# Linear attention before two mixtures of experts: keys and values laid out as head by 64 partitions

## The chip, the core and the metric

The kernel runs on one core of a Trainium2 chip. The metric is device time in microseconds, as the median of several executions. One execution is also recorded by the hardware profiler, and all rows below come from that recording. A core has a matrix engine (TensorE, PE in the rows, with its weight loads as PEld), a vector engine (VectorE, DVE), a scalar engine (ScalarE, ACT), GpSimd (POOL) and a synchronization engine (SyncE, SP) that hands out nearly all transfers. In this kernel PE's results stand in PSUM tiles and all other operands in SBUF tiles, both of up to 128 partitions.

## The reference

The inputs are float32: q, k and v of shape (4 batches, 8 heads, 576 tokens, 64), the weights of two gated layers, and domain probabilities.

```
q_s = exp(q - max over d);      q_s /= sum over d + 1e-9
k_s = exp(k - max over tokens); k_s /= sum over tokens + 1e-9
kv  = einsum('bhsd,bhse->bhde', k_s, v)
x   = einsum('bhsd,bhde->bhse', q_s, kv)      # then to (2304 tokens, 512)
y   = ((x @ w1) * (x @ w2)) @ w3 @ w_out
out = sum over 4 experts e of p[:, e] * (relu(y @ e1[e]) @ e2[e])
```

## The kernel before

All stages are in one program. A planner orders the instructions of each engine ahead of time, from the order in which the source emits them and from its own cost estimates; `hold` and `after_inst` add order edges by hand.

Attention works on pairs of heads. For a pair `(b, hp)`, `load_k` (L186, L189) brings 512 tokens as 128 partitions by four tokens for both heads side by side, and the other 64 tokens as a fifth row on 64 partitions. `load_v` does the same with a 65th column of ones, in which the sums over tokens come out. For the first batch (`V_WHOLE`) the values go through a raw buffer (L209) and a ScalarE copy (L212); for the others they are written straight into the padded tile, one transfer per head and one for the tail (L214, L217). `load_q` (L230) brings the queries as 64 partitions by nine tokens, in two transfers for each half.

`k_max` takes the maximum over the tokens of a partition on VectorE (L239, L243, L244), transposes it on PE (L246), reduces it to one column (L250), spreads that column over all partitions with a matmul against the identity (L252) and copies it out on ScalarE (L258). `k_exp` subtracts (L270) and exponentiates (L273), in two pieces, the 128-partition rows and the 64-partition tail.

`k_v` (batches 0 and 1, L294) multiplies both heads at once: five accumulating matmuls, 128 columns of weights against 130 moving columns, of which the off-diagonal blocks are thrown away. `k_v2` (batches 2 and 3, L321) does two pairs in one PSUM bank and keeps the heads apart: for each row r and head h a matmul with 64 columns of weights and 65 moving columns, so that head h writes partitions 64h to 64h+63. A float32 matmul is recorded as two passes, a transposition as one. The result is scaled into block-diagonal tiles (L308, L336), and `x_stage` (L405) applies it to the transposed queries.

Slots set the order. The first batch's attention comes ahead of all; slots 6 to 13 and 14 to 21 compute `ab_step` (L109 to L111) for the first two chunks of 512 tokens, slots 22 to 29 the product of w3 and w_out, later slots `y_step`. Batch 1's keys start at slots 6 to 9, batch 2's at 30 to 34, batch 3's at 46 to 50, between these matmuls. Meanwhile the weights, which arrive as 64-bit floats (L495), are turned into float32 on ScalarE and VectorE (`conv_abs`, L140, and `conv_rest`, L144 to L155) and split in two parts (L103, L104). The experts' layers follow (L976, L1053). In the first batch, `keep_busy` issues filler matmuls (L123).

Of the kernel before, what the change touches and what calls it, by code (L numbers as in the profile page):

```python
# [8 lines left out]
F32 = mybir.dt.float32  # L9
# [28 lines left out]
JOINED = 2  # L38
# [20 lines left out]
def linear_attention_moe_kernel(ctx: ExitStack, tc, q, k, v, w1, w2, w3, wo, dp, e1, e2, out):  # L59
# [11 lines left out]
    KR, KX = 4, S - 4 * P  # L71
# [122 lines left out]
    staged = {}  # L194

    def load_v(b, hp):
        t = ap_.tile([P, 2, KR + 1, D + 1], F32, tag="vt", name="vt", bufs=4)
        nc.gpsimd.memset(t[..., D:D + 1], 1.0)
        if b >= JOINED:
            nc.gpsimd.memset(t[KX:P, :, KR, 0:D], 0.0)  # L200
        src = v[b, 2 * hp:2 * hp + 2]
        if b in V_WHOLE:
            i = PAIRS.index(hp)
            if i % 2 == 0:
                staged[b] = raw("vs")
            x = staged[b][:, 512 * (i % 2):512 * (i % 2) + 512].rearrange(
                "p (h r d) -> p h r d", h=2, d=D
            )
            hold(("in", b), nc.sync.dma_start(  # L209
                out=x, in_=src[:, 0:KR * P].rearrange("h (p r) d -> p h r d", p=P)  # L210
            ))
            nc.scalar.activation(out=t[:, :, 0:KR, 0:D], in_=x, func=ACTF.Copy)  # L212
        for h in range(0 if b in V_WHOLE else 2):
            hold("pace" if b > 2 else ("in", b), nc.sync.dma_start(  # L214
                out=t[:, h, 0:KR, 0:D], in_=src[h, 0:KR * P].rearrange("(p r) d -> p r d", p=P)
            ))
        hold("pace" if b > 2 else ("in", b), nc.sync.dma_start(  # L217
            out=t[0:KX, :, KR, 0:D], in_=src[:, KR * P:S].rearrange("h p d -> p h d")
        ))
        vt[b, hp] = t  # L220
# [5 lines left out]
    def load_q(b, j):  # L226
        t = ap_.tile([P, 2, QR, D], F32, tag="qr", name="qr", bufs=2)
        for hh in range(2):
            h0 = 4 * hh + 2 * j
            hold("pace" if b > 2 else ("in", b), nc.sync.dma_start(  # L230
# [5 lines left out]
    def k_max(b, hp):  # L236
        kr = kraw[b, hp]
        m4 = ap_.tile([P, 2, 2, D], F32, tag="m2", name="m2", bufs=1)
        i = hold(("k", b, PAIRS.index(hp)), nc.vector.tensor_tensor(  # L239
            out=m4, in0=kr[:, :, 0:2], in1=kr[:, :, 2:4], op=ALU.max  # L240
        ))
        m2 = ap_.tile([P, 2, D], F32, tag="mf", name="mf", bufs=2)
        nc.vector.tensor_tensor(out=m2, in0=m4[:, :, 0], in1=m4[:, :, 1], op=ALU.max)  # L243
        nc.vector.tensor_tensor(out=m2[0:KX], in0=m2[0:KX], in1=kr[0:KX, :, KR], op=ALU.max)  # L244
# [4 lines left out]
        mt = ap_.tile([P, 1], F32, tag="mt", name="mt", bufs=2)  # L249
        nc.vector.tensor_reduce(out=mt, in_=ps[:, 0:P], axis=AX.X, op=ALU.max)  # L250

        i = nc.tensor.matmul(  # L252
            out=ps[:, P:2 * P], lhsT=mt.to_broadcast([P, P]), rhs=ident, start=True, stop=True
        )
        if b == 0:
            keep_busy(FILL_B[PAIRS.index(hp)], i)
        mx = ap_.tile([P, 2, 1, D], F32, tag="mx", name="mx", bufs=2)
        nc.scalar.activation(  # L258
# [921 lines left out]
```

## Time and profile before

| | |
|---|---|
| median of 3 executions | 1141.66 us (1141.65 to 1142.82) |
| the profiled execution | 1142.81 us, with a span of 1141.0 us from the first to the last instruction |
| mean granted TensorE clock over the span | 0.995 |
| PE busy | 1120.9 us, 98% of the span |
| VectorE busy | 869.1 us, 76% |
| ScalarE busy | 534.7 us, 47% |
| mean DMA rate | 270 GB/s |

The profiled execution's own time is 1.8 us above its span and 1.15 us above the median. Shares over the whole span are averages over stages with different limits. Matmul ends are modelled in the trace, so the time that a matmul takes in a stream is read from the start of one to the start of the next.

### The profile page before, as it was taken

Reading aid. Unit: us, or ns where it says so; the run is one execution under the profiler, and the core shown is the slowest. Engines: PE = TensorE matmul, PEld = TensorE weight load, DVE = VectorE, ACT = ScalarE, POOL = GpSimd, SP = SyncE. Lnnn points to the kernel's source line nnn. Section 1 sums busy time; section 2 is a strip of 40 time slices with the busy share of each in tenths; the row PEclk is TensorE's granted clock in tenths of the full one; section 3 lists DMA queues with packets and bytes.
Section 4 is the critical chain, followed back from the end, with each engine's and each line's share of the span. In section 5 each row is a group of like instructions: output and inputs, shape, how many; then the busy total and the mean of one; then the engine's idle time right before and its main releaser. Section 6 shows DMA issues by size and latency. Waiting matters only on the chain.

```text
span 1141.0 us, 18926 instructions
## 1 busy us (share of the span) xinstructions
PE 1120.9 (98%) x7159; PEld 1044.8 (92%) x7159; DVE 869.1 (76%) x1460; ACT 534.7 (47%) x974; POOL 11.4 (1%) x54
## 2 busy tenths in 40 slices
PE   7899999999999999999999999999999999999998
PEld 5677888878888889999999999999999999999998
DVE  7999696856565527999989997777779877777777
ACT  4775245745453326645555444444435434443441
POOL 0000000000010000000000000000000000000000
PEclk8999999999999999999999999999999999999999
DMA  9987962899989768777777888777777797777774
GB/s 266 269 334 289 294 174 83 222 339 396 338 283 396 301 240 311 285 281 272 290 262 289 290 305 289 248 256 251 253 253 249 251 307 249 254 251 250 253 246 128
DMA packets 124667, 308.04 MB, mean 270 GB/s; under 512 B 27936, under 2 KB 51488, under 8 KB 124576
## 3 DMA queue, kind: packets, MB, share of 16 engines
q1 hardware_dynamic: 123616, 306.04, 77.9%
q8 instruction: 57, 0.93, 0.3%
q10 hardware_dynamic: 960, 0.79, 0.3%
q14 instruction: 34, 0.28, 0.1%
HBM read 230.24 MB, written 76.55 MB: 269 GB/s over the span
## 4 chain that ended last, share of the span: by engine, by line
PE 91%; DVE 4%; DMA 3%; SPq 1%; issue 1%; ACT 0%; DVEq 0%; ACTq 0%
PE hp L976 30%; PE op L1053 29%; PE ab L111 5%; PE ab L110 5%; PE ab L109 5%; PE y L110 3%; PE y L111 3%; PE y L109 3%; PE W L109 1%; PE W L110 1%; PE W L111 1%; DMA eg<-e_b 1%; PE xp L405 1%; DMA vt<-in_v_dram 1%; PE kv L294 1%
## 5 line engine op out<-in xcount | busy, mean ns | idle before, releaser
L1053 PE MATMUL op<-eg,h 128*128 128x256 f32 x3024 | 379.8, 280 | 0.8 <-DMA eg<-e_b 0.8
L976 PE MATMUL hp<-t,eg 128*128 128x384 f32 x2016 | 376.9, 336 | 0.9 <-DVE acc L1034 0.9
L1053 PEld LDWEIGHTS op<-eg,h 128*128 128x128 f32 x3024 | 373.5, 188 | 1.2 <-PE hp L976 1.1
L976 PEld LDWEIGHTS hp<-t,eg 128*128 128x128 f32 x2016 | 344.6, 188 | 2.9 <-DVE acc L1034 1.8
L1034 DVE SCALAR_TENSOR_TENSOR acc<-op,prob,acc 128x256 f32<-128x256 f32 (+1 forms) x399 | 197.9, 525 | 42.0 <-PE op L1053 41.9
L103 ACT ACTIVATE h<-blk 128x768 fp32r<-128x768 f32 x168 | 138.0, 843 | 143.1 <-DVE blk L673 108.9
L104 DVE TENSOR_TENSOR h<-blk,h 128x768 fp32r<-128x768 f32 x168 | 157.2, 951 | 24.4 <-ACT h L103 24.3
L959 ACT ACTIVATE blk<-hp 128x384 f32<-128x384 f32 x192 | 90.4, 489 | 141.6 <-PE hp L976 138.1
L963 DVE TENSOR_TENSOR blk<-hp,blk 128x384 f32<-128x384 f32 x144 | 79.3, 556 | 67.0 <-PE hp L976 66.6
L109 PE MATMUL ab<-x,wg 128*128 128x512 f32 (+1 forms) x320 | 120.0, 378 | 1.5 <-ACT bd L308 1.1
L110 PE MATMUL ab<-x,wg 128*128 128x512 f32 (+1 forms) x320 | 118.6, 371 | 1.6 <-ACT x L426 1.4
L111 PE MATMUL ab<-x,wg 128*128 128x512 f32 (+1 forms) x320 | 117.9, 371 | 0.3 <-DVE wg L104 0.3
L965 ACT ACTIVATE blk<-blk 128x768 f32<-128x768 f32 x72 | 60.6, 845 | 73.0 <-DVE blk L963 71.3
L673 DVE TENSOR_TENSOR blk<-blk 128x768 f32<-128x768 f32 x96 | 91.4, 952 | 0.5
L110 PEld LDWEIGHTS ab<-x,wg 128*128 128x128 f32 x320 | 60.3, 189 | 13.1 <-ACT x L426 3.0
L109 PEld LDWEIGHTS ab<-x,wg 128*128 128x128 f32 x320 | 60.1, 189 | 12.7 <-ACT bd L308 1.3
L111 PEld LDWEIGHTS ab<-x,wg 128*128 128x128 f32 x320 | 60.3, 189 | 10.5 <-DVE wg L104 0.7
L567 DVE TENSOR_TENSOR ah<-ab,ah 128x512 f32<-128x512 f32 (+1 forms) x40 | 25.2, 631 | 39.3 <-PE ab L111 39.3
L104 DVE TENSOR_TENSOR eo<-e2r,eo 128x512 fp32r<-128x512 f32 x56 | 37.7, 683 | 20.0 <-ACT eo L103 19.8
L111 PE MATMUL y<-h,W 128*128 128x512 f32 x128 | 50.4, 397 | 0.0
L110 PE MATMUL y<-h,W 128*128 128x512 f32 x128 | 50.4, 394 | 0.0
L109 PE MATMUL y<-h,W 128*128 128x512 f32 x128 | 49.2, 401 | 0.0
(107 smaller groups left out, 1004.2 us busy)
## 6 DMA issues: line engine op xcount, KB each, us to landing
eg<-e_t SPq DMA_DIRECT2D x96, 512.0 KB, 4.5
eg<-e_b SPq DMA_DIRECT2D x72, 512.0 KB, 5.0
eg<-e_s SPq DMA_DIRECT2D x68, 512.0 KB, 4.4
eg<-e_a SPq DMA_DIRECT2D x51, 512.0 KB, 4.6
wg<-w SPq DMA_DIRECT2D x44, 512.0 KB, 8.3
f<-in_moe_w_dram SPq DMA_DIRECT2D x32, 512.0 KB, 6.7
e_t<-eo SPq DMA_DIRECT2D x32, 512.0 KB, 7.5
e_s<-eg SPq DMA_DIRECT2D x28, 512.0 KB, 4.5
```

The lines of the kernel that those rows point to most:

```text
L103: i = nc.scalar.activation(out=hi, in_=src, func=ACTF.Copy)
L104: j = eng.tensor_tensor(out=lo, in0=src, in1=hi.bitcast(F32), op=ALU.subtract)
L109: nc.tensor.matmul(out=ps, lhsT=w_hi, rhs=r_hi, start=first, stop=False, **kw)
L110: nc.tensor.matmul(out=ps, lhsT=w_hi, rhs=r_lo, start=False, stop=False, **kw)
L111: return nc.tensor.matmul(out=ps, lhsT=w_lo, rhs=r_hi, start=False, stop=last, **kw)
L673: return lambda: nc.vector.tensor_tensor(out=dst, in0=x, in1=y, op=op)
L959: nc.scalar.activation(out=block(name)[:, u], in_=src, func=func)
L963: nc.vector.tensor_tensor(out=x[:, u], in0=src, in1=x[:, u], op=ALU.add)
L965: nc.scalar.activation(out=x, in_=x, func=ACTF.Relu)
L976: nc.tensor.matmul(out=q, lhsT=w[:, sw, kt, P * u:P * u + P], rhs=t[b][:, kt, st], start=new and kt == 0 and i == 0, stop=kt == 1 and i == ...
L1034: nc.vector.scalar_tensor_tensor(out=dst, in0=src, scalar=prob[:, T, e:e + 1], in1=dst, op0=ALU.mult, op1=ALU.add,)
L1053: nc.tensor.matmul(out=q[:, c:c + DH], lhsT=g[:, sh, u, P * i:P * i + P], rhs=w[:, sw, u], start=new and u == 0 and j == 0, stop=u == 1 an ...
```

## The change

Keys and values are laid out as queries already are: a head takes 64 partitions, each with nine consecutive tokens, and the two heads of a pair lie on top of each other. One transfer brings the keys of a pair and one the values. The maximum over the nine tokens of a partition becomes one reduction with a stride of 64 elements. Its transposition fills 64 PSUM partitions instead of 128, the reduction to one column keeps the heads apart, and the spread takes two matmuls of 64 by 64. Subtraction and exponential become one instruction each. `k_v` and `k_v2` become one function for one or two pairs: for each of nine rows and each head, a matmul with 64 partitions of contraction, 64 columns of weights and 65 moving columns; head 0 uses partitions 0 to 63 and head 1 partitions 64 to 127, for the operands and for the result. The memsets for the tails go. The first batch's four query transfers are issued by ScalarE instead of SyncE.

```
     def load_k(b, hp):
-        t = ap_.tile([P, 2, KR + 1, D], F32, tag="kr", name="kr", bufs=4)
-        src = k[b, 2 * hp:2 * hp + 2]
+        t = ap_.tile([P, QR, D], F32, tag="kr", name="kr", bufs=4)
         hold("pace" if b > 2 else ("in", b), nc.sync.dma_start(
-            out=t[:, :, 0:KR], in_=src[:, 0:KR * P].rearrange("h (p r) d -> p h r d", p=P)
-        ))
-        hold("pace" if b > 2 else ("in", b), nc.sync.dma_start(
-            out=t[0:KX, :, KR], in_=src[:, KR * P:S].rearrange("h p d -> p h d")
+            out=t, in_=k[b, 2 * hp:2 * hp + 2].rearrange("h (p r) d -> (h p) r d", p=QP)
         ))
...
     def load_v(b, hp):
-        t = ap_.tile([P, 2, KR + 1, D + 1], F32, tag="vt", name="vt", bufs=4)
+        t = ap_.tile([P, QR, D + 1], F32, tag="vt", name="vt", bufs=4)
...
+        src = v[b, 2 * hp:2 * hp + 2].rearrange("h (p r) d -> (h p) r d", p=QP)
+        x = t[..., 0:D]
         if b in V_WHOLE:
...
+            x = raw("vs")[:, 0:QR * D].rearrange("p (r d) -> p r d", d=D)
+        hold("pace" if b > 2 else ("in", b), nc.sync.dma_start(out=x, in_=src))
+        if b in V_WHOLE:
+            nc.scalar.activation(out=t[..., 0:D], in_=x, func=ACTF.Copy)
...
-            hold("pace" if b > 2 else ("in", b), nc.sync.dma_start(
+            eng = nc.sync if b else nc.scalar
+            hold("pace" if b > 2 else ("in", b), eng.dma_start(
                 out=t[QP * hh:QP * hh + QP],
...
     def k_max(b, hp):
...
+        m2 = ap_.tile([P, D], F32, tag="mf", name="mf", bufs=2)
+        hold(("k", b, PAIRS.index(hp)), nc.vector.tensor_reduce(
+            out=m2, in_=kraw[b, hp].rearrange("p r d -> p d r"), axis=AX.X, op=ALU.max
         ))
...
-        i = nc.tensor.transpose(ps[:, 0:P], m2.rearrange("p h d -> p (h d)"), ident)
+        i = nc.tensor.transpose(ps[0:D, 0:P], m2, ident)
...
+        nc.vector.tensor_reduce(
+            out=mt, in_=ps[0:D, 0:P].rearrange("d (h p) -> d h p", h=2), axis=AX.X, op=ALU.max
+        )
+        for h in range(2):
+            i = nc.tensor.matmul(
+                out=ps[D * h:D * h + D, P:P + D], lhsT=mt[:, h].to_broadcast([D, D]),
+                rhs=ident[0:D, 0:D], start=True, stop=True,
+            )
...
+        mx = ap_.tile([P, 1, D], F32, tag="mx", name="mx", bufs=2)
+        nc.scalar.activation(out=mx[:, 0], in_=ps[:, P:P + D], func=ACTF.Copy)
...
+        t = ap_.tile([P, QR, D], F32, tag="ek", name="ek", bufs=2)
+        hold(("e", b, PAIRS.index(hp)), nc.vector.tensor_tensor(
+            out=kr, in0=kr, in1=mx.to_broadcast([P, QR, D]), op=ALU.subtract
+        ))
+        nc.scalar.activation(out=t, in_=kr, func=ACTF.Exp)
...
-    def k_v2(b, j):
...
+    def k_v(b, *pairs):
+        ps = bank(ps_w if b == 0 else ps_a, "kv").rearrange("p (w c) -> p w c", c=P)
+        n = len(pairs)
+        for w, hp in enumerate(pairs):
+            ek, vv, last = ekt.pop((b, hp)), vt.pop((b, hp)), None
+            for r in range(QR):
                 for h in range(2):
+                    p = slice(D * h, D * h + D)
                     i = nc.tensor.matmul(
-                        out=ps[D * h:D * h + D, hh, 0:D + 1], lhsT=ek[:, r, h], rhs=vv[:, h, r],
-                        start=r == 0, stop=r == KR, skip_group_check=hh > 0,
+                        out=ps[p, w, 0:D + 1], lhsT=ek[p, r], rhs=vv[p, r],
+                        start=r == 0, stop=r == QR - 1, skip_group_check=w > 0,
                     )
```

## Rows read from the trace of the kernel before

**Rows 1.** The page's first part: an engine's busy time, share of the span, instructions.

```profile
PE 1120.9 (98%) x7159; PEld 1044.8 (92%) x7159; DVE 869.1 (76%) x1460; ACT 534.7 (47%) x974; POOL 11.4 (1%) x54
```

**Rows 2.** Windows: length, each engine's busy time, granted clock, DMA share, GB/s.

```profile
3.60:16.00 12.40, 8.84 (x42) 5.95 (x41) 9.77 (x24) 3.55 (x9) 0.00 (x0) 0.89 0.96 248
16.00:46.90 30.90, 25.78 (x119) 19.11 (x118) 26.82 (x47) 23.06 (x60) 0.46 (x4) 0.88 1.09 283
46.90:75.00 28.10, 26.94 (x132) 21.70 (x131) 27.45 (x51) 21.39 (x70) 0.32 (x2) 1.00 1.04 355
75.00:92.00 17.00, 14.87 (x75) 11.31 (x74) 14.51 (x28) 11.21 (x28) 1.71 (x8) 1.00 0.60 227
92.00:340.00 248.00, 247.49 (x1251) 202.56 (x1250) 177.87 (x301) 125.19 (x255) 7.45 (x26) 1.00 0.81 271
```

**Rows 3.** Timeline of DVE, 3 to 36 us: start, us, instruction, idle before and releaser.

```profile
7.63 0.88 DVE L270 TENSOR_TENSOR kr<-kr,mx 128x512 f32<-128x512 f32 x2
8.43 0.27 DVE L244 TENSOR_TENSOR mf<-mf,kr 64x128 f32<-64x128 f32 x1
...
11.79 1.35 DVE L345 TENSOR_REDUCE qm<-qr 128x18 f32<-128x1152 f32 x1 [1.54 <-DMA qr<-in_q_dram]
...
17.93 0.16 DVE L301 TENSOR_SCALAR rs<-kv 128x1 f32<-128x1 f32 x1 [1.07 <-PE kv L294]
```

**Rows 4.** Timeline of SP's transfer issues, 0 to 110 us.

```profile
0.75 0.46 SPq L186 DMA_DIRECT2D kr<-in_k_dram  x1
...
5.94 2.56 SPq L230 DMA_DIRECT2D qr<-in_q_dram  x4
8.54 0.59 SPq L209 DMA_DIRECT2D vs<-in_v_dram  x1
```

**Rows 5.** Timeline of ACT, 0 to 17 us.

```profile
7.21 0.28 ACT L258 ACTIVATE mx<-mt 128x128 f32<-128x128 f32 x1 [4.86 <-PE mt L252]
```

**Rows 6.** DMA traffic of 8 to 12 us, then of 14 to 28 us.

```profile
DMA packets 476, 0.99 MB, mean 247 GB/s; under 512 B 47, under 2 KB 48, under 8 KB 476
...
DMA packets 5085, 4.68 MB, mean 335 GB/s; under 512 B 612, under 2 KB 5085, under 8 KB 5085
```

**Rows 7.** Groups of DVE by form, 0 to 46.9 us: busy, mean ns, idle before.

```profile
L345 DVE TENSOR_REDUCE qm<-qr 128x18 f32<-128x1152 f32 x3 | 4.0, 1344 | 1.5 <-DMA qr<-in_q_dram 1.5
...
L239 DVE TENSOR_TENSOR m<-kr 128x256 f32<-128x256 f32 x7 | 2.9, 411 | 3.7 <-DMA kr<-in_k_dram 3.7
L270 DVE TENSOR_TENSOR kr<-kr,mx 128x512 f32<-128x512 f32 x4 | 2.7, 678 | 0.0
...
L250 DVE TENSOR_REDUCE mt<-mt 128x1 f32<-128x128 f32 x5 | 1.4, 277 | 0.0
...
L270 DVE TENSOR_TENSOR kr<-kr,mx 64x128 f32<-64x128 f32 x4 | 1.1, 274 | 0.0
```

**Rows 8.** Instructions on the tile kv: duration min/median/max, first and last start.

```profile
L321 PE MATMUL kv<-vt,ek x160: 219/222/272, 181.0 to 301.5; 128*64 128x65 f32 x160
```

**Rows 9.** The chain that ended last, 198 to 204 us: start, us, what.

```profile
198.86 0.73 PE kv L321 x18
...
200.02 0.26 PE kv L321 x2
...
200.71 0.11 PE mt L246
...
203.10 0.22 PE mt L252 x2
```

**Rows 10.** Timeline of PE, 74 to 76.2 us and 232.5 to 234.8 us.

```profile
74.44 1.47 PE L294 MATMUL kv<-vt,ek 128*128 128x130 f32 x10
...
232.61 0.39 PE L110 MATMUL y<-h,W 128*128 128x512 f32 x1
232.93 1.39 PE L321 MATMUL kv<-vt,ek 128*64 128x65 f32 x40
...
234.59 0.40 PE L109 MATMUL y<-h,W 128*128 128x512 f32 x1
```

More of the change, by code (lines that the diff above doesn't have):

```diff
@@ L229, in load_q @@
             h0 = 4 * hh + 2 * j
-            hold("pace" if b > 2 else ("in", b), nc.sync.dma_start(
+            eng = nc.sync if b else nc.scalar
+            hold("pace" if b > 2 else ("in", b), eng.dma_start(
                 out=t[QP * hh:QP * hh + QP],
@@ L286, in empty_bd @@
         return bd_ring[-1]
-    def k_v(b, hp):
-        ek, vv = ekt.pop((b, hp)), vt.pop((b, hp))
-        bd = empty_bd()
-        ps = bank(ps_w if b == 0 else ps_a, "kv")
-        for r in range(KR + 1):
-            p = P if r < KR else KX
-            i = nc.tensor.matmul(
-                out=ps[:, 0:2 * D + 2], lhsT=ek[0:p, r].rearrange("p h d -> p (h d)"),
-                rhs=vv[0:p, :, r, :], start=r == 0, stop=r == KR,
-            )
-        if b == 0:
-            keep_busy(FILL_V[PAIRS.index(hp)], i)
-        rs = ap_.tile([P, 1], F32, tag="rs", name="rs", bufs=2)
-        nc.vector.tensor_scalar(
-            out=rs, in0=ps[:, D:D + 1], scalar1=1e-9, scalar2=None, op0=ALU.add
-        )
-        nc.vector.reciprocal(out=rs, in_=rs)
-        for h in range(2):
-            p = slice(D * h, D * h + D)
-            o = (D + 1) * h
-            nc.scalar.activation(
-                out=bd[p, D * h:D * h + D], in_=ps[p, o:o + D], func=ACTF.Copy, scale=rs[p]
-            )
-        kvb[b, hp] = bd
-    def k_v2(b, j):
-        ps = bank(ps_a, "kv").rearrange("p (w c) -> p w c", c=P)
-        bds, last = [], None
-        for hh in range(2):
-            bds.append(empty_bd())
-            ek, vv = ekt.pop((b, 2 * hh + j)), vt.pop((b, 2 * hh + j))
-            for r in range(KR + 1):
+    def k_v(b, *pairs):
[4 more added lines that the diff above has]
+            for r in range(QR):
                 for h in range(2):
+                    p = slice(D * h, D * h + D)
                     i = nc.tensor.matmul(
-                        out=ps[D * h:D * h + D, hh, 0:D + 1], lhsT=ek[:, r, h], rhs=vv[:, h, r],
-                        start=r == 0, stop=r == KR, skip_group_check=hh > 0,
+                        out=ps[p, w, 0:D + 1], lhsT=ek[p, r], rhs=vv[p, r],
+                        start=r == 0, stop=r == QR - 1, skip_group_check=w > 0,
                     )
@@ L327, in k_v2 @@
                     last = i
-        rs = ap_.tile([P, 2, 1], F32, tag="rs2", name="rs", bufs=2)
+        if b == 0:
+            keep_busy(FILL_V[PAIRS.index(hp)], i)
+        rs = ap_.tile([P, n, 1], F32, tag=f"rs{n}", name="rs", bufs=2)
         nc.vector.tensor_scalar(
-            out=rs, in0=ps[:, 0:2, D:D + 1], scalar1=1e-9, scalar2=None, op0=ALU.add
+            out=rs, in0=ps[:, 0:n, D:D + 1], scalar1=1e-9, scalar2=None, op0=ALU.add
         )
         nc.vector.reciprocal(out=rs, in_=rs)
-        for hh in range(2):
+        for w, hp in enumerate(pairs):
+            kvb[b, hp] = empty_bd()
             for h in range(2):
@@ L336, in k_v2 @@
                 nc.scalar.activation(
[L337 removed]
+                    out=kvb[b, hp][p, p], in_=ps[p, w, 0:D], func=ACTF.Copy, scale=rs[p, w]
                 )
[L339 removed]
     def q_exp(b, j):
@@ L456, in linear_attention_moe_kernel @@
             elif i % 2:
-                put(mid, s + 1, k_v2, b, i // 2)
+                put(mid, s + 1, k_v, b, PAIRS[i - 1], hp)
             at = s + (4 if b > 1 else 3)
```

50 lines of the change are left out of this document (1 added, 49 removed).

## The prediction

> **What bounds the kernel now.** I read the page's first part, then windows, then inside the stages the timelines, groups and chain. PE is busy for 98% of the span [rows 1], but a mean hides the start. The windows [rows 2] show four stages. From 3.6 to 46.9 us VectorE is busy for 36.59 of 43.30 us and PE has holes at a lower clock: attention of the first batch and the first weight conversions, in VectorE's order. From 46.9 to 75 us VectorE (27.45 of 28.10) and PE (26.94) are both nearly full. From 75 to 92 us PE misses 2.1 us. After that PE is the limit: in 92 to 340 us it lacks 0.51 us of 248, with VectorE at 72%. So a saving counts only up to about 92 us, where VectorE and the arrival of data set the pace; later everything that PE gains or loses goes to the end one for one. Batches 2 and 3 lie wholly in that later stage: their products run from 181 to 301 us [rows 8].
>
> **VectorE, per pair.** Durations come from [rows 7]. Before: 411 (L239), two of about 277 (L243, L244, like L250), 277 (L250), 678 and 274 (L270), in sum 2.19 us. After: one reduction over 576 elements, the small one, one subtraction over 576. Reductions cost 277 ns for 128 elements and 1344 for 1152, so 1.04 ns an element and 0.74 us for 576; subtractions 274 for 128 and 678 for 512, so 0.75 us for 576. With 0.28 that makes 1.77 us, 0.42 less. But durations overlap: the two L270 record 0.88 us and the next instruction starts 0.80 after them [rows 3], 0.08 per boundary, and three instructions fewer lose 3 x 0.08 of the gain. So 0.18 to 0.42 us, taken as 0.3. Batch 0 saves 4 x 0.3 = 1.2 us. Batch 1's 1.2 us falls mostly into 46.9 to 75, where PE is as full as VectorE and has only 1.16 us of holes [rows 2]; I count 0.4.
>
> No row has the stride of 64 elements. The reduction can't well be below the 0.74 us of a contiguous one; above, I take twice that. I choose 0.74, and the doubled price is a rival. The Trainium skill, "SBUF — State Buffer", section "Door 1: The DMA port swizzle", says that an access which moves on to another 16-byte line pays a penalty; no row here shows such a stride.
>
> **Transfers and queues.** SyncE now needs twelve issues before the first values: eight for keys from 0.75 us, four for queries from 5.94, so that the first value transfer goes at 8.54 [rows 4]. With four key transfers and the queries on ScalarE, at the same 0.64 us each (2.56 / 4), the values go at about 0.75 + 4 x 0.64 = 3.3 us and the first query at about 0.8 us. ScalarE's four issues cost 2.6 us and are hidden: before its first copy of the maximum, at 7.21 us, it has been idle for 4.86 [rows 5]. Without that cover they would add up to 2.6 us to the first pair's chain. Later batches save one key and two value issues a pair; PE doesn't wait there.
>
> What goes away are two of VectorE's waits [rows 3]: 1.54 us for the queries before 11.79 and 1.07 us for the first pair's product, which itself waits for values, before 17.93. Together 2.6 us. I count them fully, because queries and values are asked for over 5 us sooner. The first keys may land later, beside the queries; I set that against the short waits between the key transfers, at zero.
>
> DMA's share is 0.96 from 3.6 to 16 us and 1.09 to 46.9 [rows 2], so what comes earlier pushes other transfers back. The rate depends on the shape: 247 GB/s while query pieces of 2304 bytes dominate, 335 with pieces of 1 KB [rows 6]. New key and value transfers have pieces of 2304 bytes but all 128 partitions, where the queries have 64. By the slow rate 295 KB takes 1.19 us, by the other 0.88; over the twelve such transfers of the first two batches that is at most 12 x 0.31 = 3.7 us later at the end of this stage, and at least none. I take none, as the transfers that a wait names are the first ones. The Trainium skill, "SBUF — State Buffer", section "Door 1: The DMA port swizzle", has 64 partitions reach only half of the 16 ports, 128 all: by that rule the new layout isn't slow and the sum stays; if the size of the pieces were the cause, it would be up to 3.7 us worse. The trace holds no 2304-byte transfer on 128 partitions.
>
> So the start gains 1.2 + 0.4 + 2.6 = 4.2 us. Bounds: nothing, if the waits come back elsewhere or the planner's new order costs as much; and 10.1 us, all 6.7 us of VectorE's idle time to 46.9 (43.30 less 36.59 [rows 2]) and 8 x 0.42 of its work.
>
> **PE, the products of batches 2 and 3.** Here the work grows. Per function call the old code issues 2 pairs x 5 rows x 2 heads x 2 passes = 40, the new one 2 x 9 x 2 x 2 = 72: with 64 partitions a matmul covers half as many tokens. The chain gives 0.73 us for 18 passes and 0.26 for 2 [rows 9]: 0.47 / 16 = 29 ns a pass. A pass of L252 with 128 moving columns takes 0.11 us [rows 9], so 65 columns alone would take about 56 ns: the two heads run side by side, 58 ns for both. The new code keeps two heads on disjoint halves, so I keep 58. It needs 36 such steps for 20: 16 x 0.058 = 0.93 us a call, four calls, 3.7 us.
>
> Entering and leaving such a group costs too. Around the 40 passes the wide matmuls start at 232.61 and 234.59 [rows 10]: 1.98 us, less 0.46 for two wide ones at 0.23 each, less 20 x 0.058, leaves 0.36 us of overhead. Batch 1's product is a group of 36 passes now: 18 x 0.058 + 0.36 = 1.40 us, as against 1.47 [rows 10]; no change.
>
> **PE, the maximum.** The two passes of L252 take 0.22 us in the stream and the transposition 0.11 [rows 9], with no overhead visible. The spread becomes two 64-by-64 matmuls, thus a small group: 0.36 + 2 x 0.058 = 0.48 us, 0.26 more. Were there no overhead, it would be 0.11 less. The transposition has 64 columns of weights: between nothing and the same overhead, up to 0.3 more; between ends without a near row I take half, 0.15. Eleven pairs meet a full PE, eight of batches 2 and 3 and about three of batch 1: 11 x 0.41 = 4.5 us, bounds -1.2 and 6.2.
>
> Rescaling (L301, L329) and the copies to the diagonal keep their number. ScalarE's exponential and copy get about 0.3 us a pair shorter; ScalarE is at 74% before 46.9 and at half after, so that is worth nothing. The dropped memsets lie on GpSimd, busy 0.46 us of 30.9 [rows 2].
>
> **The sum.** 3.7 + 4.5 - 4.2 = +4.0 us, PE's part between 2.5 and 9.9, the start's between 0 and 10.1. Against the profiled execution, 1142.8 us with 1.8 around its span, this is 1146.8; that execution lies 1.15 us above the median, so against the median it is 1145.7. I forecast 1145.5 us, 0.3% slower. I call 0.2%, 2.3 us, the least that measurement can tell here.
>
> **Rivals.**
>
> A, the forecast: the start gains a few microseconds and PE pays about twice that. For it speak the windows after 92 us, where nothing can hide a longer PE. Chance 0.44, with times of 1143.5 to 1149.
>
> B, not slower: small groups pay no entry or exit where the maximum is spread and turned. Then PE's part is 2.5 us, the sum -1.7 and the time 1140.0. For it: L252 in the stream shows no overhead. Against: L321's groups do, at the same number of columns. It decides where the sum is zero: 11 x (1.5 x overhead - 0.10) = 0.5, at an overhead of 0.10 us a group, half of it counted for the transposition. Chance 0.22; it turns into faster if the start gains over 4.8 us.
>
> C, the start moves as a block: queries and values come over 5 us sooner and everything behind them follows, 5.3 us, with 2.4 of VectorE's work and the 2.1 us that PE lacks from 75 to 92, together 9.8. Less 8.2 for PE that is -1.6, 1140.1 us; with PE nearer to its lower bound it is below 1139.4 and faster. For it: the first product waits for its values. Against: VectorE is 87% busy from 16 to 46.9 us, and DMA is full. It decides at a gain of 8.2 us. Chance 0.18.
>
> D, the start gains about 1 us: either the strided reduction costs 0.74 us more (8 x 0.74 = 5.9, more than the gain), or keys land later beside the queries. Time 1141.7 + 8.2 - 1 = 1148.9. Chance 0.12.
>
> E, the two heads don't run side by side: 72 passes at 56 ns, 4.0 us instead of 20 x 0.058 = 1.2 a call, 11.5 for four, and 1.0 more for each of batch 1's four: 15.4 instead of 3.7, so about 1157 us. The Trainium skill, "TensorEngine Tiling (Array Packing)", section "Gotcha 1: PSUM Pressure", says that different row tiles can't access one PSUM bank at the same time, and here both heads' rows write one bank. Against it: they write different partitions of it, as the two heads do now, side by side. Chance 0.04.
>
> **Range and chances.** From C's faster part at about 1138.5 to D with some more, 1150; outside lie E and the ends of the bounds, under 2 in 10. Slower: 0.42 of A, 0.10 of D and E, 0.56. Faster: 0.09 of B and 0.13 of C, 0.22. Same: the rest of each, 0.22. The likeliest case's own range is 1143.5 to 1149.
>
> **What the profile would show.** The first query reduction starts well before 11.8 us, and no wait of 1 us for a product stands near 18. The reduction over 576 elements takes 0.74 us. In batches 2 and 3 a product has 72 passes with starts in pairs, 58 ns from pair to pair, and takes about 2.5 us in the stream. The spread takes 0.48 us instead of 0.22. The last hole of PE lies some 4 us earlier than 92. The prediction is wrong if the start gains more than 8 us, if the spread costs no more than before, or if the planner's new order opens holes in PE after 92 us.

## The result and the profile after

The changed kernel takes 1150.42 us (median of 6 runs, 1148.64 to 1153.40), the kernel before 1141.66 beside it (6 runs, 1141.24 to 1142.82): ratio 1.0078, 95% interval 1.0063 to 1.0092. It is slower by 8.8 us, where 3.8 were forecast, and 0.4 us outside the range. The profiled execution of after took 1149.19 us with a span of 1147.1. The traces thus differ by 6.4 us; the other 2.4 of the medians lie between executions of one kernel, and no trace locates them: the trace of before is the slowest of its six executions, that of after the second fastest, so by traces the new kernel looks a little better than it is.

I divide the trace by three events on TensorE: the first wide product (tile `ab`), the first product of `w_out` (W from `wg`), the first expert product (`hp`). In the expectations times count from a zero 0.24 us earlier: 108.77 there is 108.5 here; stretches are the same.

| | first `ab` | first W | first `hp` | W to `hp` |
|---|---|---|---|---|
| before | 32.3 | 108.8 | 424.3 | 315.5 |
| after | 34.8 | 108.5 | 430.3 | 321.8 |

From `hp` to the last product both take 711.5 to 711.7 us. So the start gained 0.3 us of the 3.0 forecast for it (4.2 less 3 x 0.41 for batch 1's maxima), and the stretch with batches 2 and 3 lost 6.3 of a forecast 7.0. The tiles W and `hp` of after, then of before; the last pair of numbers is the first and last start:

```profile
L108 PE MATMUL W<-wg x64: 388/389/500, 108.5 to 198.4; 128*128 128x512 f32 x64
```

```profile
L924 PE MATMUL hp<-t,eg x2016: 334/334/446, 430.3 to 1113.6; 128*128 128x384 f32 x184
```

```profile
L109 PE MATMUL W<-wg x64: 389/389/500, 108.8 to 198.0; 128*128 128x512 f32 x64
...
L976 PE MATMUL hp<-t,eg x2016: 332/334/445, 424.3 to 1107.9; 128*128 128x384 f32 x184
```

The page's first part and the windows of after, as [rows 1, 2]:

```profile
PE 1123.1 (98%) x7527; PEld 1044.4 (91%) x7527; DVE 874.2 (76%) x1412; ACT 532.3 (46%) x958; POOL 7.8 (1%) x38
```

```profile
3.60:16.00 12.40, 7.33 (x57) 4.25 (x57) 9.16 (x12) 3.35 (x7) 0.00 (x0) 1.00 1.06 288
16.00:46.90 30.90, 23.91 (x220) 17.48 (x217) 30.23 (x45) 21.32 (x54) 0.49 (x4) 0.94 1.07 307
46.90:75.00 28.10, 27.27 (x193) 21.58 (x191) 27.26 (x46) 23.23 (x75) 0.23 (x2) 1.00 1.00 333
75.00:92.00 17.00, 15.91 (x132) 12.59 (x131) 12.75 (x24) 10.22 (x24) 0.23 (x2) 1.00 0.57 206
92.00:340.00 248.00, 245.96 (x1360) 199.11 (x1359) 177.28 (x267) 118.84 (x236) 1.87 (x10) 1.00 0.78 262
```

VectorE's idle time from 3.6 to 46.9 us fell from 6.7 [rows 2] to 43.30 - 39.39 = 3.9 us, 2.8 us less where the forecast counted 2.6. But it is not the forecast's two waits that went. The one for the first product did (1.07 us); the one for the queries stayed (1.82 us, 1.54 before) and only stands 2.5 us earlier. The rest are mainly two waits for ScalarE, before 29.31 and 35.88 us of before's trace (0.95 and 1.09). That the sums agree is luck. The 2.8 us of work done sooner did not become time at W: from 75 to 92 us VectorE idles 4.25 us against 2.49. Its new groups up to 46.9 us (busy, mean ns, idle before) and its timeline, against [rows 3, 7]:

```profile
L218 DVE TENSOR_REDUCE mf<-kr 128x64 f32<-128x576 f32 x8 | 9.1, 1142 | 4.2 <-DMA kr<-in_k_dram 4.2
...
L243 DVE TENSOR_TENSOR kr<-kr,mx 128x576 f32<-128x576 f32 x5 | 3.7, 744 | 0.0
```

```profile
9.26 1.35 DVE L293 TENSOR_REDUCE qm<-qr 128x18 f32<-128x1152 f32 x1 [1.82 <-DMA qr<-in_q_dram]
...
18.16 0.15 DVE L277 TENSOR_SCALAR rs<-kv 128x1 f32<-128x1 f32 x1
...
19.69 0.68 DVE L143 TENSOR_SCALAR f<-f 128x1024 f32<-128x1024 f32 x1
```

Two rows of before's timelines, of VectorE and of ScalarE:

```profile
20.67 0.69 DVE L144 TENSOR_SCALAR f<-f 128x1024 f32<-128x1024 f32 x1
```

```profile
14.82 0.63 ACT L212 ACTIVATE vt<-vs 128x512 f32<-128x512 f32 x1 [3.86 <-DMA vs<-in_v_dram]
```

The subtraction costs the forecast 0.74 us. The strided reduction costs 1.14, not 0.74, so a pair records 2.16 us against 2.19: no saving. The first query reduction is 2.5 us earlier (11.79 before), the first conversion step L143 only 1.0 (20.67 before). In between stand arrivals. SyncE's issues (as [rows 4]), its own waits up to 60 us, and ScalarE's timeline:

```profile
0.74 2.23 SPq L184 DMA_DIRECT2D kr<-in_k_dram  x4
5.41 0.33 SPq L196 DMA_DIRECT2D vs<-in_v_dram  x1
...
9.18 2.76 SPq L196 DMA_DIRECT2D vs<-in_v_dram  x3
```

```profile
SPq L196 <- DMA qr<-in_q_dram: 6.1, 3, 2.4
```

```profile
13.78 0.68 ACT L198 ACTIVATE vt<-vs 128x576 f32<-128x576 f32 x1 [0.55 <-DMA vs<-in_v_dram]
...
20.45 0.69 ACT L139 ACTIVATE f<-f 128x512 f32<-128x512 f32 x1 [0.83 <-DMA f<-in_moe_w_dram]
...
30.05 1.25 ACT L139 ACTIVATE f<-f 128x512 f32<-128x512 f32 x2 [1.03 <-DVE wg L103]
31.18 1.16 ACT L312 ACTIVATE qe<-qr 128x1152 f32<-128x1152 f32 x1
32.37 0.49 ACT L342 ACTIVATE qT<-qt 128x384 f32<-128x384 f32 x1
```

With four key and four query transfers asked for, SyncE's next issue waits until a query has landed (the trace doesn't show why): the first values go at 5.41 us, not 3.3, the others from 9.18. Their first copy starts at 13.78, 1.0 us earlier than before (14.82), though they were asked for 3.1 us earlier; DMA's share there is 1.06. At 20.45 ScalarE waits for a weight.

On TensorE, around the last product call and around one spread of a maximum:

```profile
306.28 0.39 PE L110 MATMUL y<-h,W 128*128 128x512 f32 x1
306.60 2.32 PE L267 MATMUL kv<-vt,ek 64*64 64x65 f32 x72
308.84 0.50 PE L108 MATMUL y<-h,W 128*128 128x512 f32 x1
309.18 0.40 PE L109 MATMUL y<-h,W 128*128 128x512 f32 x1
```

```profile
211.58 0.39 PE L110 MATMUL y<-h,W 128*128 128x512 f32 x1
211.90 0.33 PE L230 MATMUL mt<-ident,mt 64*64 64x64 f32 x4
212.16 0.50 PE L108 MATMUL y<-h,W 128*128 128x512 f32 x1
212.50 0.40 PE L109 MATMUL y<-h,W 128*128 128x512 f32 x1
```

A group's cost in the stream is the time from the start of the wide product ahead to the start of the second one behind, less two wide ones at 0.227. The 72 passes cost 309.18 - 306.28 - 0.45 = 2.44 us, 1.52 before for 40 by the same sum; the spread costs 0.47, 0.225 before; the transposition 0.12, as before (269.23 to 269.80 us there).

### The profile page after: what moved, and what is told of

Same layout as the page of the kernel before. It is cut to its first block, busy times and chain, and to the rows that moved or that the text cites. A ratio compares the mean times of both kernels' runs of the same rounds, so it can differ in the third digit from the quotient of the medians.

```text
span 1147.1 us, 19509 instructions
## 1 busy us (share of the span) xinstructions
PE 1123.1 (98%) x7527; PEld 1044.4 (91%) x7527; DVE 874.2 (76%) x1412; ACT 532.3 (46%) x958; POOL 7.8 (1%) x38
## 4 chain that ended last, share of the span: by engine, by line
PE 90%; DVE 5%; DMA 3%; issue 1%; ACT 0%; ACTq 0%; DVEq 0%; SPq 0%
PE hp L924 29%; PE op L1001 29%; PE ab L108 5%; PE ab L110 5%; PE ab L109 5%; PE y L108 3%; PE y L110 3%; PE y L109 3%; PE W L108 1%; PE W L109 1%; PE W L110 1%; PE xp L353 1%; DMA eg<-e_b 1%; PE kv L267 1%; DMA kr<-in_k_dram 1%
## 5 line engine op out<-in xcount | busy, mean ns | idle before, releaser
L103 DVE TENSOR_TENSOR eo<-e2r,eo 128x512 fp32r<-128x512 f32 x56 | 37.9, 685 | 20.5 <-ACT eo L102 20.2
```

What stands on the lines that cost most here:

```text
L103: j = eng.tensor_tensor(out=lo, in0=src, in1=hi.bitcast(F32), op=ALU.subtract)
```

## The experiments

Each median stands beside runs of before on the same chip. "Order fixed" means added edges that give every engine the changed kernel's own sequence of instructions; in the other kernels the planner makes a new one.

| | median, us (runs) | ratio, 95% | first `ab` | first W | W to `hp` |
|---|---|---|---|---|---|
| hybrid | 1143.83 (10) | 1.0007 to 1.0026 | 34.7 | 108.4 | 316.0 |
| tree | 1152.09 (4) | 1.0076 to 1.0110 | 35.9 | 111.1 | 320.9 |
| q_on_sync | 1152.70 (4) | 1.0075 to 1.0105 | 34.6 | 108.5 | 322.7 |
| old_q_scalar | 1144.84 (10) | 1.0013 to 1.0032 | 36.1 | 110.2 | 315.5 |
| order | 1153.18 (4) | 1.0071 to 1.0109 | 32.5 | 110.0 | 321.9 |
| hybrid_order | 1146.15 (7) | 1.0022 to 1.0045 | 33.1 | 110.4 | 316.0 |
| tree_order | 1149.99 (4) | 1.0050 to 1.0080 | 35.4 | 110.1 | 320.5 |
| old_order | 1143.63 (10) | 1.0002 to 1.0020 | 36.3 | 109.6 | 315.8 |
| few_rows_max | 1150.19 (4) | 1.0045 to 1.0090 | 33.7 | 111.5 | 321.9 |
| max_twice | 1156.23 (4) | 1.0099 to 1.0138 | 39.7 | 113.3 | 323.5 |
| few_values | 1153.15 (4) | 1.0070 to 1.0110 | 37.2 | 112.1 | 322.7 |
| fixed_few_rows | 1148.41 (4) | 1.0042 to 1.0070 | 34.9 | 107.9 | 322.5 |
| fixed_in_a_row | 1149.27 (4) | 1.0047 to 1.0074 | 34.3 | 107.7 | 322.6 |
| fixed_exp_first | 1149.13 (5) | 1.0052 to 1.0076 | 34.5 | 108.5 | 322.3 |
| one_spread | 1154.62 (4) | 1.0073 to 1.0122 | 35.6 | 112.1 | 325.3 |
| one_piece | 1147.99 (5) | 1.0040 to 1.0066 | 34.8 | 108.1 | 320.2 |
| before_one_piece | 1141.98 (12) | 0.9989 to 1.0007 | 31.1 | 108.6 | 314.2 |
| fixed_three | 1147.09 (6) | 1.0038 to 1.0063 | 34.6 | 108.8 | 319.8 |

**hybrid: the new layout in batches 0 and 1, the old one in 2 and 3.**

```
     def k_max(b, hp):
+        if b >= JOINED:
+            return k_max_old(b, hp)
...
-                put(mid, s + 1, k_v, b, PAIRS[i - 1], hp)
+                put(mid, s + 1, k_v2, b, i // 2)
```

(so too `load_k`, `load_v` and `k_exp`.)

> The changed kernel for batches 0 and 1, the code of before for batches 2 and 3 (layout, maximum, exponential, product). Theory on PE: the longer time comes from 16 more passes steps per product and from small groups of 64-column tiles in batches 2 and 3, where PE is full: 6.3 us between the first W and the first hp. So that stretch returns from 321.8 to 315.5 us, the start stays as in the changed kernel (first W at 108.8), and the time is about 1144. Rival: the stretch got longer because of what batches 0 and 1 left behind (order of the planner, late transfers); then it stays above 319 us.

The stretch returns to 316.0 us and the median falls by 6.6 from after's. So TensorE's part is 5.8 to 6.6 us and lies in batches 2 and 3. What is left is the new start alone: by the trace (the fastest of its ten executions) 0.4 us earlier than before's at W, by medians (1143.83 against 1142.29) 1.5 us slower. It gains nothing. hybrid also settles a rival that the profiles suggest, TensorE's clock, whose granted mean over the start differs from trace to trace (its two levels are 1.2 and 2.4 GHz). Up to W its VectorE, ScalarE and TensorE carry out after's instructions in after's order; its granted clock is 0.69 from 3.6 to 16 us and 0.90 to 46.9, after's 1.00 and 0.94, and its W still comes 0.1 us earlier.

**Three causes for the start, one at a time.** tree takes the maximum over rows pairwise, without a stride; q_on_sync gives the first queries back to SyncE; old_q_scalar is the kernel before with only the queries on ScalarE.

```
-        hold(("k", b, PAIRS.index(hp)), nc.vector.tensor_reduce(
-            out=m2, in_=kraw[b, hp].rearrange("p r d -> p d r"), axis=AX.X, op=ALU.max
-        ))
+        hold(("k", b, PAIRS.index(hp)), nc.vector.tensor_tensor(
+            out=m4, in0=kr[:, 0:4], in1=kr[:, 4:8], op=ALU.max
+        ))
+        nc.vector.tensor_tensor(out=m4[:, 0:2], in0=m4[:, 0:2], in1=m4[:, 2:4], op=ALU.max)
...
-            eng = nc.sync if b else nc.scalar
+            eng = nc.sync
```

> The changed kernel, with the strided reduction of the keys replaced by a tree of four contiguous maxima (256, 128, 64, 64 elements). Two theories for why the first 109 us gained only 0.3 us instead of 4.2. Stride: the reduction over a stride of 64 elements takes 1.12 us instead of the 0.74 forecast, and VectorE paces the start. By the other durations the tree takes 0.41 + 0.28 + 0.21 + 0.21 less 3 x 0.08 of overlap, 0.87 us, against 1.12: 0.25 less for each of eight pairs, so the first product of the weights (W) starts about 2 us earlier, at 106.8 instead of 108.8, and the time falls to about 1148.4. Queue: the start is set by the values and queries, whose transfers wait for each other; then the tree moves the first W by less than 0.7 us. PE's part between 109 and 430 us should stay (321.8 us from the first W to the first hp) by both.

> The changed kernel, with the first batch's query transfers handed out by SyncE again, behind the keys. Queue theory: with the queries on ScalarE the keys land later (the second pair's at 6.1 us) and the value transfers wait for the queries to land (three waits of 6.1 us in all), so this brings the keys earlier; the values are issued at about 5.9 instead of 5.4 and 9.2 us, and the first W starts 0.5 to 2 us earlier. Stride theory: VectorE is full from 16 to 47 us either way, and the first W moves by less than 0.5 us, or gets later by up to 1.5 because the queries land later. From the first W to the first hp 321.8 us by both.

> The kernel before, with only the first batch's queries handed out by ScalarE. Queue theory: the queries slow the keys, and the values wait for them; the first W starts at 109 us or later, no gain, although VectorE's wait of 1.5 us for the queries is smaller. Forecast's view, that the queries and values were late because of SyncE's issues: the first W starts 1 to 2.6 us earlier, at 106.4 to 108, and the time falls to 1139 to 1140.6. From the first W to the first hp 315.5 us by both.

tree's first W comes 2.6 us later, not earlier, with VectorE waiting 6.9 us for keys up to W, 4.2 in after. q_on_sync leaves W where it was, so no effect of the queue shows at W in the new layout; in the old layout, with its eight key transfers, moving the queries costs 1.4 us at W and 2.5 in the median, the planner's new order included.

**The planner's order.** In after the second queries' exponential on ScalarE comes at 31.18 us behind absolute values of a weight conversion (above; 28.12 before), and the first wide product comes 2.5 us later than before's. order adds edges that put it, and then the normalization on VectorE, first; the three others carry the same edges on other kernels.

```
-AFTER_Q = {(0, 1): [("q", 1, 0)]}
+AFTER_Q = {(0, 1): [("q", 1, 0), ("k", 1, 0), ("k", 1, 1), ("conv", 2)]}
...
+        if (b, j) == (0, 1):
+            gate["abs", 2] = [i]
```

> The changed kernel, with order edges that bring back the order of before in one place: the exponential of the second query group goes ahead of the absolute values of weight job 2 on ScalarE, and the normalization of these queries ahead of job 2's conversion and of the first two key maxima of batch 1 on VectorE. Order theory: the changed kernel's start gains nothing because the planner fills VectorE's and ScalarE's earlier time with job 2 (done at 37.9 instead of 44.7 us) while the queries' exponential, which the first chunk of x needs, comes at 31.2 instead of 28.1 us. Then the exponential comes at 28.5 to 29.5, the first product with w1 and w2 at 32 to 33 instead of 35.0, the first W 1.5 to 2.5 us earlier than 108.8, and the time falls by about 2 us, to 1148.5. VectorE theory: it has as much work as before and paces all; then the first W moves by less than 0.7 us.

> New layout in batches 0 and 1, code of before in batches 2 and 3, with the order edges. Order theory: the start gains about 2 us on the hybrid (first W at about 106.6 instead of 108.6), the time is about 1141.8 and no slower than before. VectorE theory: as the hybrid, first W at 108 to 109, about 1143.8.

> The same order edges with the tree of contiguous maxima in place of the strided reduction. The tree alone brought the first W to 111.35 us, 2.6 later than the changed kernel, in spite of less work on VectorE. Order theory: with the order held, the tree's shorter work counts, and the first W comes 0.5 to 2 us before that of the run with the order edges alone. If the tree's loss has another cause (more instructions and waits on the keys), the first W stays behind that run by 1 us or more.

> The kernel before with its first queries handed out by ScalarE, and the order edges. Without the edges its first W came at 110.5 us, 1.4 later than before. Order theory: the edges bring it back to 108 to 109 or earlier, and the time from 1144.8 to at most 1142.8. If the queries on ScalarE themselves do the harm, by slowing the keys and values, the first W stays at 110 or later.

The edges did what they say: the first wide product came at 32.5 us. But W came 1.5 us later than in after; VectorE then waits 3.83 us for ScalarE before 67.94 us. The theory that this place is where the gain went fell here. The edges cost hybrid 2.0 us of W as well. With the tree W comes at 110.1, 1.0 earlier than tree's and no earlier than order's. In old_order they bring W from 110.2 to 109.6 and the median to 1143.63, not down to the 1142.8 that the order theory expects.

**Is it VectorE's work or what arrives?** Two of nine rows in the maxima of batches 0 and 1; the maximum taken twice; one of nine value rows loaded.

```
-            out=m2, in_=kraw[b, hp].rearrange("p r d -> p d r"), axis=AX.X, op=ALU.max
+            out=m2, in_=kraw[b, hp][:, 0:QR if b > 1 else 2].rearrange("p r d -> p d r"),
+            axis=AX.X, op=ALU.max
```

```
+        if b < 2:
+            nc.vector.tensor_reduce(
+                out=m2, in_=kraw[b, hp].rearrange("p r d -> p d r"), axis=AX.X, op=ALU.max
+            )
```

```
+        m = QR if b > 1 else 1
+        if m < QR:
+            nc.gpsimd.memset(x[:, m:QR], 0.0)
...
-nc.sync.dma_start(out=x, in_=src)
+nc.sync.dma_start(out=x[:, 0:m], in_=src[:, 0:m])
```

> The changed kernel, but in batches 0 and 1 the key maximum is taken over two of the nine rows of a partition (the exponentials are then shifted by another number). Takes some 0.8 us (1.14 to about 0.3) from VectorE eight times, 6.6 us. Theory V, VectorE's work sets the pace up to the first product of w_out at 108.77 us: that product comes 4 to 6.6 us earlier, near 103, and the time falls to about 1144 to 1146. Rival T, the arrival of transfers sets it: within 1 us of 108.8 and within 1.5 of 1150.4. Rival B, VectorE, TensorE and transfers are in balance and a saving on one is stopped by the others: 1 to 3 us earlier, 1147.5 to 1149.5.

> The changed kernel with the strided reduction of batches 0 and 1 issued twice (the second result is the one used): 8 x 1.14 = 9.1 us more of VectorE. V: the first product of w_out 6 to 9 us later than 108.77, the time 1156.5 to 1159.5. T: up to 2 us later, under 1152.5. B: a cost on an engine that is nearly full isn't given back, 4 to 9 us later: B is told from V by the kernel with fewer rows, not by this one.

> The changed kernel, but in batches 0 and 1 only one of the nine value rows of a partition is loaded (the other eight are zeros written by GpSimd): 8 x 262 KB = 2.1 MB less to transfer, 6 to 7 us at the 283 to 340 GB/s of these stages. V: no transfer that VectorE waits for is among them, the first product of w_out within 1.5 us of 108.77, time within 1.5 of 1150.4. T: 4 to 6 us earlier, 1144.5 to 1146.5. B: 1 to 3 us earlier, 1147.5 to 1149.5.

Neither less work (6.6 us) nor fewer bytes (2.1 MB) made the start earlier: W came 3.0 and 3.6 us later. More work (9.1 us) made it 4.8 us later, between T and V, as B has it. All three theories of a single bound miss on the first and the third kernel; but the planner had made a new order for each, so durations and order are mixed (few_values also has a lower granted clock, 0.65 and 0.70 in the first two windows).

**Durations alone, order fixed.** fixed_few_rows is few_rows_max so; fixed_in_a_row replaces the stride by nine neighbours.

```
-            out=m2, in_=kraw[b, hp].rearrange("p r d -> p d r"), axis=AX.X, op=ALU.max
+            out=m2, in_=kraw[b, hp].rearrange("p r d -> p d r") if b > 1
+            else kraw[b, hp].rearrange("p r d -> p (r d)").rearrange("p (d r) -> p d r", r=QR),
+            axis=AX.X, op=ALU.max
```

> As few_rows_max (two of nine rows in the key maximum of batches 0 and 1), with the order of every engine's and queue's instructions up to the first product of w_out fixed to that of the changed kernel, so that only durations differ. A reduction takes 0.29 us in few_rows_max, against 1.14: 8 x 0.85 = 6.8 us less of VectorE. Theory V, the reduction's price set the start and the planner's order hid it in few_rows_max: the first product of w_out comes some 4.5 us earlier than 108.77 (batch 0 whole, batch 1 a third), near 104, time near 1146. Rival Q, what VectorE saves is taken up by waits for data and for TensorE in any order: 107 to 109 us, time within 1.5 of 1150.4.

> The changed kernel in its own fixed order, with the reductions of batches 0 and 1 over nine neighbours instead of a stride of 64 (a maximum over other elements of the same keys, which shifts the exponentials by another number per column): the contiguous reduction that the prediction priced, 0.74 us. It takes 0.74 if the stride is what costs 1.14, and 1.14 if it is the nine-element groups. V: 8 x 0.4 = 3.2 us less, first product of w_out 1.6 to 2.2 us earlier, near 106.8. Q: within 1 us of 108.77.

The group of VectorE in fixed_in_a_row:

```profile
L218 DVE TENSOR_REDUCE mf<-kr 128x64 f32<-128x576 f32 x8 | 6.0, 745 | 4.9 <-DMA kr<-in_k_dram 4.9
```

745 ns is the price that the prediction chose; 1142 with the stride. So it is the stride that costs 0.4 us. Yet 8 x 0.4 = 3.2 us less brings W only 0.9 us earlier, and 8 x 0.86 = 6.9 us less only 0.6. Half of that can be chance: one_piece (below), whose start is after's, has W 0.45 us earlier. Instruction by instruction against after, VectorE's lead in fixed_few_rows is 1.28 us at 20 us, 0.47 at 24, 1.66 at 47 and 0.6 from 60 us to W. What takes it stands in ScalarE's timeline of that kernel:

```profile
13.85 0.68 ACT L198 ACTIVATE vt<-vs 128x576 f32<-128x576 f32 x1 [1.57 <-DMA vs<-in_v_dram]
...
20.47 0.67 ACT L139 ACTIVATE f<-f 128x512 f32<-128x512 f32 x1 [0.80 <-DMA f<-in_moe_w_dram]
```

Both start within 0.1 us of after's (13.78, 20.45), however early VectorE is: values and weights have not landed. (In fixed_in_a_row they land 0.5 us earlier, 13.29 and 19.96.) The 0.9 us left over at W in fixed_in_a_row goes too. VectorE waits there for batch 2's queries, which land no earlier than in after; its timeline in after, then in fixed_in_a_row:

```profile
140.79 1.35 DVE L293 TENSOR_REDUCE qm<-qr 128x18 f32<-128x1152 f32 x1 [2.45 <-DMA qr<-in_q_dram]
```

```profile
141.23 1.35 DVE L295 TENSOR_REDUCE qm<-qr 128x18 f32<-128x1152 f32 x1 [3.77 <-DMA qr<-in_q_dram]
```

The lead of 0.9 us before that landing is a lag of 0.4 behind it, and TensorE meets it some 30 us later. Its timeline in fixed_in_a_row:

```profile
171.64 0.73 PE L110 MATMUL W<-wg 128*128 128x512 f32 x2 [0.51 <-DVE wg L103]
```

This product starts at 171.85 us in after. TensorE waits there for a weight conversion on VectorE, and both fixed kernels have only 0.1 to 0.2 us of lead behind it. Rival Q holds.

**One place of ScalarE's order, all else fixed.** The exponential (31.18) and the copy (32.37) stand ahead of the absolute values (30.05).

```
 ACT  bd<-kv,rs x2
-ACT  f<-f x2 (L139)
 ACT  qe<-qr (L312)
 ACT  qT<-qt (L342)
+ACT  f<-f x2 (L139)
 ACT  x<-xp
```

> The changed kernel with its whole order fixed, but for ScalarE: the exponential of the second queries and the copy of their transposition (31.18 and 32.37 us in the changed kernel's trace) stand ahead of the two absolute values of a weight conversion (30.05), which wait 1.03 us for VectorE. Theory O, this place in the planner's order is where the start's gain was lost (TensorE waits 3.05 us there for the copy, and its first wide product starts at 35.02 instead of 32.53 us): first wide product near 32.9, first product of w_out 1.5 to 2.2 us earlier, near 107, time near 1148.6. Rival Q, the lead is taken up before 109 us: first wide product near 32.9, first product of w_out within 0.7 us of 108.77.

TensorE's timeline in it:

```profile
30.95 1.24 PE L353 MATMUL xp<-qT,bd 128*128 128x288 f32 x4 [0.92 <-ACT qT L342]
...
34.29 0.37 PE L370 MATMUL xp<-x,nident 128*128 128x224 f32 x1 [1.50 <-ACT x L369]
```

The products of L353 start 1.96 us earlier than in after (32.91), but the next ones then wait 1.50 us for ScalarE's copy of x. The first wide product gains 0.3 us, W 0.1. Q again.

**TensorE's groups.** one_spread spreads both maxima with one matmul of 64 rows and 128 columns.

```
+        nc.scalar.activation(out=mw, in_=mt.to_broadcast([D, 2, D]), func=ACTF.Copy)
+        i = nc.tensor.matmul(
+            out=ps[:, P:P + D], lhsT=mw.rearrange("d h c -> d (h c)"), rhs=ident[0:D, 0:D],
...
```

> The changed kernel with the maxima copied by ScalarE to a tile of 64 x 128 and spread by one matmul of 64 rows and 128 columns in place of two of 64 x 64. The spread took 0.465 us in the stream, against 0.225 for the old one with 128 rows. Theory C, the overhead is that of two matmuls on halves of the columns: it falls to 0.11 to 0.24 us, and the stretch from the first product of w_out to the first expert product (321.8 us) falls by 8 x 0.23 to 0.35 = 1.8 to 2.8 us. Rival R, it is that of a matmul on half of the rows: it stays at 0.4 or more, and the stretch within 0.8 us of 321.8. The start is the same for both but for the planner's order; the time follows the stretch.

TensorE's timeline in it, around one spread among wide products:

```profile
262.27 0.39 PE L110 MATMUL ab<-x,wg 128*128 128x512 f32 x1
262.58 0.43 PE L231 MATMUL mt<-ident,mw 64*128 64x64 f32 x2
...
263.29 0.39 PE L109 MATMUL ab<-x,wg 128*128 128x512 f32 x1
```

Full columns don't take the overhead away: 263.29 - 262.27 - 0.45 = 0.57 us, more than the 0.47 of after for half as many passes. So C falls. But half the rows (R) is not the whole rule either. Before's own products use all 128 rows on 64 columns, and six of their passes cost 193.47 - 192.44 - 0.45 = 0.58 us, of which three steps at 0.058 explain 0.17. TensorE's timeline of before:

```profile
192.44 0.39 PE L111 MATMUL y<-h,W 128*128 128x512 f32 x1
192.75 0.45 PE L321 MATMUL kv<-vt,ek 128*64 128x65 f32 x6
...
193.47 0.40 PE L110 MATMUL W<-wg 128*128 128x512 f32 x1
```

Beside their passes, groups on half the rows, on half the columns or on both pay an estimated 0.35 to 0.45 us; only the transposition, a single pass of 128 rows on 64 columns, shows none, and why is open. The stretch grew by 3.5 us: 2.49 are one wait of TensorE for VectorE (at 345.55 us), in the planner's new order, and eight dearer spreads make 0.8.

Pieces are also in after. Its timeline within that call, which is broken in seven:

```profile
199.20 0.79 PE L267 MATMUL kv<-vt,ek 64*64 64x65 f32 x18
199.93 0.50 PE L489 MATMUL W<-W,nident 128*128 128x512 f32 x1
200.35 0.33 PE L267 MATMUL kv<-vt,ek 64*64 64x65 f32 x2
200.61 0.50 PE L489 MATMUL W<-W,nident 128*128 128x512 f32 x1
201.04 0.44 PE L267 MATMUL kv<-vt,ek 64*64 64x65 f32 x6
```

one_piece moves its passes together, in an order otherwise fixed; before_one_piece does so with the four pieces of before.

```
-PE  kv x7, kv x2, kv x9, kv x1, kv x3, kv x7, kv x7 (instructions, two passes each)
+PE  kv x36
```

> The changed kernel with its whole order fixed, but for the 72 passes of the first product call of batch 2, which stand in one piece where the last of their seven pieces stood. Theory G, each piece pays the entry of a small group: the pieces cost 5.6 us in the stream and one piece 2.44, so the stretch from the first product of w_out to the first expert product falls from 321.8 by 3.1 us to 318.7, the time to about 1147.3. Rival H, the pieces fill holes in which TensorE would wait anyway: the stretch within 0.7 us of 321.8.

> The kernel before with its whole order fixed, but for the 40 passes of the first product call of batch 2, in one piece instead of four. G: 2.97 us in the stream become 1.52, the stretch falls from 315.5 to 314.1, the time by 1.4 to about 1140.8. H: within 0.5 us of before.

```profile
198.93 2.32 PE L267 MATMUL kv<-vt,ek 64*64 64x65 f32 x72
```

The stretch falls by 1.6 us, the first expert product comes 2.1 us earlier; around the call itself TensorE gains 2.1 us. That is G, at half of its size by the stretch and two thirds by the call. The median is 2.4 us below after's, but only 0.4 to 1.3 below those of fixed_few_rows, fixed_in_a_row and fixed_exp_first, which ran on the same chip: about half of the 2.4 is not the piece's. My 5.6 us for the pieces counted an entry twice where one wide product stands between two pieces; by the lead of the products around them they cost 4.6. In before the stretch falls by 1.3 us, but the median is the same (ratio 0.9998): 0.1% is not resolved there.

fixed_three has ScalarE's order, the contiguous reduction and the one piece together.

> The changed kernel in its fixed order with three edits together: ScalarE's order as in fixed_exp_first, the contiguous reduction of fixed_in_a_row (first product of w_out 0.9 us earlier there), and the 72 passes in one piece as in one_piece (stretch 1.6 us shorter there). If they add: first product of w_out near 106 (O) or 107.5 (Q), stretch near 320.2, time 1145.5 to 1147.5. If the waits that they remove hide one another: no better than the best of the three alone, 1148.

The stretch is the shortest of the kernels with the new layout throughout (319.8). W is not earlier at all (108.8): the weight that ScalarE waits for lands at 21.68 us there, 1.2 later than in after, and takes VectorE's lead of 1.0. The median is 3.3 us below after's, 2.0 to 2.2 below those of fixed_in_a_row and fixed_exp_first, 0.9 below one_piece's. On TensorE the edit counts, in the start the two others don't. No kernel of the study beats the one before.

## Why the prediction was wrong

The sign was right, TensorE's part nearly so. The step that failed is "So the start gains 1.2 + 0.4 + 2.6 = 4.2 us": it gained 0.3 at W, where the forecast leaves 3.0. With the measured 0.25 us for each of batch 1's three maxima, that is an estimated 1.0 for the 4.2.

- **The reduction.** "I choose 0.74" for the stride of 64 was 0.4 us too little: 1.14, between the choice and rival D's doubled price. With it the 1.2 + 0.4 us of VectorE's work are nothing: a pair takes 2.16 us for 2.19. The rule cited there, the Trainium skill, "SBUF — State Buffer", section "Door 1: The DMA port swizzle", is borne out: elements 256 bytes apart cost 1142 ns for 576, neighbours 745. But fixed_in_a_row shows that this is worth at most 0.9 us at W, a third of what is missing, and nothing at the first expert product.
- **The two waits, 2.6 us "counted fully".** VectorE idles 2.8 us less, but by luck: the wait for the product went, that for the queries stayed (1.82 us) and two for ScalarE made up the sum. The lead at the first query reduction was 2.5 us. But one wait is not the gate: values and weights land at 13.8 and 20.5 us, in fixed_few_rows too, where VectorE is 1.3 us earlier, and 1.0 us of lead was left there. The assumption that values are asked for over 5 us sooner missed SyncE's wait for the queries (5.41 and 9.18 us).
- **"So a saving counts only up to about 92 us", and there whole.** It counts little there. With the order held, 6.9 us less of VectorE's work gave 0.6 us at W. Where no engine waits long, each hands its gain on to the next one's wait: for values, weights, ScalarE's copies. And TensorE waits for VectorE as late as 171.6 us, so the stage after 92 us is not TensorE's alone.
- **The planner's new order.** few_rows_max has W at 111.5 us in the planner's order and at 107.9 in after's: the order is 3.6 us there. In tree and few_values (W 2.6 and 3.6 us later) order and work are not separated. The prediction named a costly new order as one way to the bound "nothing". The outcome lay near that bound, but that after's order lost time to before's was not shown: the new layout was never run in before's order. Why each order comes out as it does was not settled either.
- **The product, 3.7 us.** Right in mechanism: heads run side by side (72 passes in 2.32 us, 64 ns a pair with its entry), +0.92 us a call as forecast 0.93. Between the starts of products its passes take 4.0 us more in batches 2 and 3. The pieces of the first call, which the term left out, take 4.6 us instead of 2.5; in before they took 1.3 to 1.5 too much already, so 0.6 to 0.8 us is new. The Trainium skill, "TensorEngine Tiling (Array Packing)", section "Gotcha 1: PSUM Pressure", does not hold here, and rival E with it.
- **The maximum, 0.41 us a pair.** The spread cost 0.24 more (0.26 forecast), the transposition nothing, not 0.15. Eight pairs thus cost 1.9 us for 3.3 forecast. Rival B is wrong: the spread pays its entry.
- **The rivals.** C, the start as a block, is as wrong as the sum's own start. D comes nearest (1148.9 us): its gain of about 1 us is what the start's trace shows. But the stride costs half of D's price, and with the order held it explains 0.9 us at most; the rest is the landings and waits, so D's size is right for another reason.
- **What the profile would show.** The last hole of TensorE before 109 us was to lie some 4 us earlier than 92; it lies at 97.05 us, 0.99 us for VectorE, where before has its last at 90.36. So TensorE still waits for VectorE 6.7 us later than in before.

## What to carry over

A wait that goes away is worth what the next gate lets through: list the landings that stand behind it, and take the smallest lead among them, not the sum of the idle times. Where several engines are nearly full, work that is taken away buys almost nothing (6.9 us gave 0.6 with the order held), while work that is added can cost (9.1 gave 4.8, though in a new order), so a mixed change is safer priced near its costs. And where a planner orders the instructions, fix the order before an experiment on durations: without it few_rows_max, with less work, came out 3.0 us later, and read like evidence.

## What was not expected of the hardware

- The entry to a group of matmuls on part of the array costs whichever side is halved: one_spread's two passes on 64 rows by 128 columns cost 0.57 us, after's four on 64 by 64 0.47, before's six on 128 by 64 0.58, while before's two on 128 by 128 cost 0.225. A single transposition on 128 rows by 64 columns cost 0.12, as on 128 by 128.
- Removing 2.1 MB of early transfers (few_values) did not make the start earlier, although DMA's share is over 1 to 46.9 us; in another order and at a lower clock, so it isn't shown that bytes don't matter.
